# Bank width of ScalarE's softmax reads, and the durations in a list scheduler, in a two-layer attention kernel

## Chip, cores, metric

One core of one Trainium2 chip. The metric is device time in microseconds (us), median of the executions of a kernel. Each ratio compares runs of one job on one chip. One run of the kernel before, of 6325 us (granted clock 1.0), is marked slow and is left out everywhere. PE is the tensor engine, ScalarE is ACT in the profile, VectorE is DVE.

## The reference, cut

```python
def _A_ref(x, wq, wk, wv, wo):             # S=2048, D=512, 32 query heads of 16, one K/V head
    q = split_heads(x @ wq); k = x @ wk; v = x @ wv
    p = softmax(einsum("bhqd,bkd->bhqk", q, k) * 16 ** -0.5)
    return merge(einsum("bhqk,bkd->bhqd", p, v)) @ wo
# _B_ref: linear attention with a feature map phi, 32 heads of 16
x = x + _A_ref(layernorm(x), ...); x = x + _B_ref(layernorm(x), ...)   # this pair twice
```

The two A blocks hold nearly all the work: 2 x 32 x 2048 x 2048 exponentials, which is 4096 score blocks of 128 x 512. The rest (projections, transposes, normalisation, block B) is 222 small jobs per layer that each need a bank, and the kernel slides most of them in between the score blocks.

## The kernel before: the parts that matter

The kernel is built by its own list scheduler. At build time it simulates five engines with a duration for each operation. Whenever an engine is free in that simulation, it takes the ready operation of the best priority. The outcome is a fixed instruction order for each engine, with semaphore waits. That order is fixed in the program: **the durations cost no time, they only shape the order.**

```python
SHARE = True
def tdv(n, c=1.04): return 0.065 + n * c * 1e-3      # VectorE, us for n columns
def tac(n):         return 0.09 + n * 0.833e-3       # ScalarE
```

All matmuls of the profile write to one tensor, `ps_all`, which the kernel allocates in PSUM and divides into eight banks of 512 columns. Banks 0-2 and 3-5 are two "sets" for ScalarE: PE writes a score block into each bank of a set, then one ScalarE exp reads the whole set while PE refills the other. Bank 6 serves both VectorE's score blocks (kind "x") and all small jobs; bank 7 accumulates the output. With `SHARE`, small jobs may also take bank 5, and then the second set is only two banks wide:

```python
# Banks.take(kind), for a small job
elif f[6]: got = 6
elif f[5] and self.share(): got = 5          # share(): SHARE and not ramp and not tail
# Ctl.step(): fill a set
for s in ((0,) if self.ramp else (0, 1)):
    w = 3
    if s == 1 and SHARE and (not banks.free[5] or (not banks.free[6] and self.waiting())):
        w = 2
    ...
# Ctl.fill(): refill by PE, then the exp by ScalarE
o  = add(PE, 0.05 + 0.14 * m, ..., prio=0.0, name="sA")
oe = add(AC, tac(m * 512), lambda e: e.activation(PTA[...], bank(3 * s, m * 512), ACTF.Exp, scale=SCALE), ...)
# Ctl.dstep(): VectorE takes a block farther ahead, if bank 6 is free; if a small job waits, they alternate
if not banks.free[6] or self.dhold(): return False
if self.dlast and self.waiting():     return False
```

So each score block goes to ScalarE (source line L775) or to VectorE (L829 reads bank 6; L846 to L851 make an exp by bit tricks, two blocks at a time), as the simulation decides. Where PE would idle, the scheduler adds filler matmuls (L897).

The softmax here doesn't subtract the row's maximum and nothing guards it: scores larger than these inputs give would overflow.

## Time and profile before

| | before |
|---|---|
| median time | 1849.07 us (3 runs, 1846.9 to 1851.51) |
| busy: PE / ScalarE / VectorE | 95% / 94% / 90% |
| score blocks: ScalarE / VectorE | 3573 / 523 |
| ScalarE exps three / two / one wide | 1039 / 227 / 2 |

Groups by line with shapes kept apart. Columns: count, busy us, mean ns of one as recorded, then the idle time just before them and what ended it.

```profile
L775 ACT ACTIVATE PTA<-ps_all 128x1536 bf16<-128x1536 f32 x1039 | 1437.1, 1478 | 57.6 <-PE ps_all L635 50.7
...
L829 DVE TENSOR_SCALAR xT<-ps_all 128x512 int32<-128x512 f32 x523 | 358.8, 686 | 48.9 <-PE ps_all L635 45.7
...
L775 ACT ACTIVATE PTA<-ps_all 128x1024 bf16<-128x1024 f32 x227 | 235.5, 1038 | 1.7 <-PE ps_all L635 1.4
L897 PE MATMUL ps_all<-maskx,zer 128*128 128x512 bf16 x594 | 205.0, 387 | 0.0
```

The recorded length of an exp (1478 ns on average for three banks) is not what it costs: neighbours overlap. I therefore took, from the trace's records, the time from each exp's start to the next ScalarE instruction's start. At best it is 1330 ns for three banks and 903 ns for two. The means are 1375 and 1171 ns (here and in the tables cut to whole ns). A three-wide exp is usually followed on time (median 1330 ns); one of two banks, on average 268 ns late.

Windows of a burst of small jobs, of a quiet stretch, and of another burst (columns as the first line says):

```profile
core 0: us, PE busy (x) PEld busy (x) DVE busy (x) ACT busy (x) POOL busy (x), PEclk, DMA share, GB/s
450.00:525.00 75.00, 73.54 (x464) 21.64 (x460) 64.74 (x123) 69.38 (x64) 2.60 (x4) 1.00 0.00 1
525.00:650.00 125.00, 119.99 (x709) 31.49 (x709) 118.57 (x200) 120.91 (x92) 0.00 (x0) 1.00 0.00 1
675.00:750.00 75.00, 72.87 (x458) 21.28 (x456) 59.98 (x117) 70.18 (x64) 4.47 (x5) 1.00 0.00 1
```

In the bursts ScalarE is busy 69.4 and 70.2 of 75 us and VectorE only 64.7 and 60.0; in the quiet stretch ScalarE is busy 97% and VectorE 95%. Most two-wide exps lie in bursts. The waits, in us, times and longest, show ScalarE and VectorE each held up by PE's score matmuls:

```profile
engine line waited for: us in total, times, longest us
...
ACT PTA L775 <- PE ps_all L635: 52.1, 127, 1.5
DVE xT L829 <- PE ps_all L635: 45.7, 88, 1.5
```

### The profile page before, as it was taken

The page shows a single profiled execution, that of the slowest core. Times are in us where ns is not written, and L with a number is a line of the kernel's source. Part 1 is how long each engine was busy: PE and PEld are TensorE (multiplying, and loading weights), DVE is VectorE, ACT ScalarE, POOL GpSimd, SP SyncE. Part 2 cuts the span into 40 slices and gives each one's busy share as a digit, 9 for nine tenths or more (in the row PEclk, how much of TensorE's full clock was granted, in tenths as well). Part 3 has the DMA queues.
Part 4 walks back from the last instruction along what each step waited for, and adds up shares of the span by engine and source line. Part 5 has one row for each costly group of instructions (what it writes and reads, how often), then busy time and mean ns, then how long its engine had stood idle before and what let it go on. Part 6 is the DMA issues. An engine that isn't in the chain of part 4 may idle for free.

```text
span 1845.4 us, 26741 instructions
## 1 busy us (share of the span) xinstructions
PE 1754.5 (95%) x11002; PEld 515.1 (28%) x11002; DVE 1658.7 (90%) x2966; ACT 1739.9 (94%) x1529; POOL 34.2 (2%) x46
## 2 busy tenths in 40 slices
PE   7999999999999999999899999999999999999998
PEld 3222222222222222223342222222223222232224
DVE  7999988999889997998689999899997999989985
ACT  7999999999999999999699999999999999999996
POOL 0000000000000000000000000000000000000000
PEclk9999999999999999999999999999999999999999
DMA  3000000000000000000000000000000000000001
GB/s 115 1 1 1 1 1 1 1 1 1 1 1 1 1 1 1 1 1 1 1 1 1 1 1 1 1 1 1 1 1 1 1 1 1 1 1 1 1 1 46
DMA packets 7722, 9.08 MB, mean 5 GB/s; under 512 B 1456, under 2 KB 7088, under 8 KB 7600
## 3 DMA queue, kind: packets, MB, share of 16 engines
q1 hardware_dynamic: 7600, 7.37, 1.2%
q8 instruction: 86, 1.41, 0.3%
q14 instruction: 36, 0.29, 0.1%
HBM read 5.28 MB, written 2.10 MB: 4 GB/s over the span
## 4 chain that ended last, share of the span: by engine, by line
PE 44%; DVE 43%; ACT 11%; issue 1%; POOL 1%; DMA 0%; SPq 0%
PE ps_all L635 17%; PE ps_all L671 13%; ACT PTA L775 10%; DVE xT L829 9%; DVE PTD L851 8%; PE ps_all L496 7%; DVE xs L850 5%; DVE xs L847 5%; DVE xu L846 4%; DVE xu L849 3%; DVE xs L848 2%; PE ps_all L897 2%; PE ps_all L692 1%; DVE Eo L683 1%; DVE stats L461 1%
## 5 line engine op out<-in xcount | busy, mean ns | idle before, releaser
L775 ACT ACTIVATE PTA<-ps_all 128x1536 bf16<-128x1536 f32 (+1 forms) x1268 | 1640.6, 1398 | 59.4 <-PE ps_all L635 52.1
L635 PE MATMUL ps_all<-QT,Kr 64*128 64x512 bf16 x4096 | 835.1, 383 | 42.0 <-DVE xT L829 16.0
L671 PE MATMUL ps_all<-PTA,Vaug 128*32 128x512 bf16 x3573 | 539.3, 389 | 3.4 <-DVE Eo L683 2.8
L829 DVE TENSOR_SCALAR xT<-ps_all 128x512 int32<-128x512 f32 x523 | 358.8, 686 | 48.9 <-PE ps_all L635 45.7
L851 DVE SCALAR_TENSOR_TENSOR PTD<-xT,xs 128x1024 uint16<-128x1024 int32 (+1 forms) x262 | 318.4, 1215 | 1.4
L635 PEld LDWEIGHTS ps_all<-QT,Kr 64*128 64x128 bf16 x4096 | 175.2, 93 | 500.9 <-ACT PTA L775 198.2
L671 PEld LDWEIGHTS ps_all<-PTA,Vaug 128*32 128x32 bf16 x3573 | 129.5, 93 | 463.4 <-issue 451.5
L897 PE MATMUL ps_all<-maskx,zer 128*128 128x512 bf16 x594 | 205.0, 387 | 0.0
L846 DVE TENSOR_SCALAR xu<-xT 128x1024 f16<-128x1024 uint16 (+1 forms) x262 | 180.2, 688 | 3.0
L850 DVE TENSOR_TENSOR xs<-xs,xu 128x1024 f16<-128x1024 f16 (+1 forms) x262 | 179.0, 684 | 3.0
L847 DVE TENSOR_TENSOR xs<-xu 128x1024 f16<-128x1024 f16 (+1 forms) x262 | 178.7, 682 | 2.0
L671 PE MATMUL ps_all<-PTD,Vaug 128*32 128x512 bf16 x523 | 144.3, 385 | 16.4 <-DVE Eo L683 12.9
L848 DVE TENSOR_SCALAR xs<-xs 128x1024 f16<-128x1024 f16 (+1 forms) x262 | 109.6, 418 | 2.1
L849 DVE TENSOR_SCALAR xu<-xu 128x1024 f16<-128x1024 f16 (+1 forms) x262 | 109.5, 418 | 0.0
L897 PEld LDWEIGHTS ps_all<-maskx,zer 128*128 128x128 bf16 x594 | 48.7, 96 | 105.0 <-issue 98.3
L496 PE MATMUL ps_all<-wqkv_sb,xnT 128*128 128x512 bf16 x256 | 70.9, 383 | 3.3 <-DVE xnT L485 1.1
L469 POOL TENSOR_TENSOR rstd<-veps,mhalf 128x1 f32<-128x1 f32 x30 | 30.7, 1025 | 1731.1 <-DVE veps L467 1723.3
L940 DVE TENSOR_SCALAR e_buf<-e_buf 128x512 f32<-128x512 f32 x64 | 26.9, 422 | 32.8 <-ACT e_buf L939 32.5
L671 PEld LDWEIGHTS ps_all<-PTD,Vaug 128*32 128x32 bf16 x523 | 32.3, 94 | 65.3 <-DVE Eo L683 27.7
L692 PE MATMUL ps_all<-identf,Eo 128*128 128x128 f32 x256 | 42.0, 287 | 5.6 <-DVE Eo L683 4.0
L939 ACT ACTIVATE e_buf<-ps_all 128x512 f32<-128x512 f32 x64 | 39.0, 610 | 8.3 <-PE ps_all L496 6.1
L461 DVE BATCH_NORM_STATS2 stats<-x_sb 128x6 f32<-128x512 bf16 x64 | 43.2, 683 | 3.3 <-DMA x_sb<-in_A_x_dram 2.6
(87 smaller groups left out, 841.6 us busy)
## 6 DMA issues: line engine op xcount, KB each, us to landing
out_dram<-x_sb SPq DMA_DIRECT2D x16, 128.0 KB, 1.7
x_sb<-in_A_x_dram SPq DMA_DIRECT2D x3, 512.0 KB, 6.7
wqkv_sb<-in_B_wqkv_dram SPq DMA_DIRECT2D x1, 1536.0 KB, 11.6
x_sb<-in_A_x_dram SPq DMA_DIRECT2D x2, 256.0 KB, 3.1
wq_sb<-in_A_wq_dram SPq DMA_DIRECT2D x1, 512.0 KB, 4.6
wo_sb<-in_A_wo_dram SPq DMA_DIRECT2D x1, 512.0 KB, 8.5
wo_sb<-in_B_wo_dram SPq DMA_DIRECT2D x1, 512.0 KB, 10.9
wk_sb<-in_A_wk_dram SPq DMA_DIRECT2D x1, 16.0 KB, 2.6
```

The lines of the kernel that those rows point to most:

```text
L496: i = e.matmul(bank(h.idx, n), lhsT=l, rhs=r, start=(c + k == 0), stop=(c + k == len(mms) - 1))
L635: x = e.matmul(bank(b0 + k), lhsT=Kr[r, m, kt * P:(kt + 1) * P], rhs=QT[r, self.units[u][0] % 2, gs, q0:q0 + n], start=True, stop=True)
L671: return e.matmul(ps[32 * c:32 * c + 32, 7 * 512:8 * 512], lhsT=Vaug[:, kt, :], rhs=src, start=opened[0], stop=opened[1], skip_group_check ...
L775: oe = add(AC, tac(m * 512), lambda e: e.activation(PTA[:, hp.idx, 0:m * 512], bank(3 * s, m * 512), ACTF.Exp, scale=SCALE), deps=[o] + pr ...
L829: o = add(DV, tdv(512), lambda e: e.tensor_scalar(out=xT[:, hx.idx, i * 512:(i + 1) * 512], in0=bank(6), scalar1=SCALE * LOG2E * 65536.0, ...
L846: o = add(DV, tdv(w, 0.52), lambda e: e.tensor_scalar(out=u_, in0=lo, scalar1=1.0 / 65536, scalar2=-0.5, op0=ALU.mult, op1=ALU.add), deps= ...
L847: o1 = add(DV, tdv(w, 0.52), lambda e: e.tensor_tensor(out=s_, in0=u_, in1=u_, op=ALU.mult), deps=[o] + c["prev"], name="xsq", **kw)
L848: o2 = add(DV, tdv(w, 0.26), lambda e: e.tensor_scalar(out=s_, in0=s_, scalar1=XK, scalar2=-XW, op0=ALU.mult, op1=ALU.add), deps=[o1], nam ...
L849: o3 = add(DV, tdv(w, 0.26), lambda e: e.tensor_scalar(out=u_, in0=u_, scalar1=1.0, scalar2=XL, op0=ALU.mult, op1=ALU.add), deps=[o1], nam ...
L850: o4 = add(DV, tdv(w, 0.52), lambda e: e.tensor_tensor(out=s_, in0=s_, in1=u_, op=ALU.mult), deps=[o2, o3], name="xc", **kw)
L851: o5 = add(DV, tdv(w), lambda e: e.scalar_tensor_tensor(out=PTD[:, hp.idx, 0:w].bitcast(U16), in0=xT[:, k, 0:w], scalar=2.0 ** -9, in1=s_, ...
L897: o = add(PE, 0.03 + FILLN * 0.41e-3, lambda e: e.matmul(bank(7, FILLN), lhsT=zer[:], rhs=maskx[:].bitcast(BF16)[:, 0:FILLN], start=not ow ...
```

## The change

Its intent: ScalarE always reads three banks (bank 5 is no longer lent), and the scheduler's durations are set to what the chip shows. `tac` is the duration of an exp and of ScalarE's few small operations. The core of the diff:

```diff
-    SHARE = True
+    SHARE = False
-        return 0.065 + n * c * 1e-3          # tdv, VectorE
+        return 0.068 + n * c * 1e-3
-        return 0.09 + n * 0.833e-3           # tac, ScalarE
+        return 0.0525 + n * 0.8325e-3
 # and seven lines with single durations, cut: bn_aggr 0.18 -> 0.09; veps 0.14 -> 0.062; transposed copies 0.4 -> 0.333 (twice);
 # K evacuation +0.06 (VectorE) and +0.1 (ScalarE); reciprocal 0.246 -> 0.168; zb 0.13 -> 0.195
```

More of the change, by code (lines that the diff above doesn't have):

```diff
@@ L461, in layer_norm @@
         add(DV, tdv(512), lambda e: e.bn_stats(stats[:, t, 0:6], x_sb[:, t, :]), reads=[("x", t)], writes=[("st", t)], prio=prio, name="bn")
-        add(DV, 0.18, lambda e: e.bn_aggr(mv[:, t, :], stats[:, t, 0:6]), reads=[("st", t)], writes=[("mv", t)], prio=prio - 0.01)
+        add(DV, 0.09, lambda e: e.bn_aggr(mv[:, t, :], stats[:, t, 0:6]), reads=[("st", t)], writes=[("mv", t)], prio=prio - 0.01)
         if ctl.ramp or ctl.tail:
@@ L466, in layer_norm @@
         else:
-            add(DV, 0.14, lambda e: e.tensor_scalar(out=veps[:, t:t + 1], in0=mv[:, t, 1:2], scalar1=1e-5, scalar2=None, op0=ALU.add),
+            add(DV, 0.062, lambda e: e.tensor_scalar(out=veps[:, t:t + 1], in0=mv[:, t, 1:2], scalar1=1e-5, scalar2=None, op0=ALU.add),
                 reads=[("mv", t)], writes=[("ve", t)], prio=prio - 0.02)
@@ L485, in cp @@
             return f(xnT[:, :, t * P:(t + 1) * P], bank_bf(hb.idx))
-        o2 = add((DV, AC), {DV: 0.4, AC: tac(512)}, cp, deps=[o], uses=[hb], rel=[hb] + ([win] if win else []), writes=[("xnT", t)], prio=prio - 0.04, name="xnT", cb=cb)
+        o2 = add((DV, AC), {DV: 0.333, AC: tac(512)}, cp, deps=[o], uses=[hb], rel=[hb] + ([win] if win else []), writes=[("xnT", t)], prio=prio - 0.04, name="xnT", cb=cb)
     def proj(h, mms, n, reads, prio, chunk=2, name="proj"):
@@ L513, in k_proj @@
                 ops = {}
-            ops[m] = add((DV, AC), {DV: tdv(b - a), AC: tac(b - a)}, ev, deps=[o] + ([ops[m - 1]] if m else []), uses=[h], rel=[h] if m == NM - 1 else [],
+            ops[m] = add((DV, AC), {DV: 0.06 + tdv(b - a), AC: 0.1 + tac(b - a)}, ev, deps=[o] + ([ops[m - 1]] if m else []), uses=[h], rel=[h] if m == NM - 1 else [],
                          reads=["mpar"], writes=[("K", m, t) for t in range(t0, t0 + n)], prio=prio - 0.05, name="kev")
@@ L694, in norm @@
             o = add(PE, 1.0, tr, reads=["identf"], deps=[oe], acq=[ht, hos] if par == 0 else [ht], uses=[he], rel=[he], prio=1.2, name="trA")
-            o = add(DV, 0.246, lambda e: e.reciprocal(rden[:, hr.idx, :].unsqueeze(2), bank(ht.idx).rearrange("p (a c) -> p a c", c=32)[:, :, DH:DH + 1]),
+            o = add(DV, 0.168, lambda e: e.reciprocal(rden[:, hr.idx, :].unsqueeze(2), bank(ht.idx).rearrange("p (a c) -> p a c", c=32)[:, :, DH:DH + 1]),
                     deps=[o], acq=[hr], uses=[ht], prio=0.0, name="recA")
@@ L921, in cp @@
             return fn(OT[:, :, g, :] if fine else OT[:, g, :, :], bank_bf(h.idx))
-        o2 = add((DV, AC), {DV: 0.4, AC: tac(512)}, cp, deps=[o], uses=[h], rel=[h], writes=keys, prio=pr, name="otc")
+        o2 = add((DV, AC), {DV: 0.333, AC: tac(512)}, cp, deps=[o], uses=[h], rel=[h], writes=keys, prio=pr, name="otc")
         if fine:
@@ L1021, in kv_block @@
                 for g in (2 * hh, 2 * hh + 1):
-                    add(DV, tdv(P, 0.52), lambda e, g=g: e.tensor_scalar(out=zb[:, g, :], in0=maskx[:, 0:P], scalar1=zf[:, g:g + 1], scalar2=None, op0=ALU.mult),
+                    add(DV, 0.195, lambda e, g=g: e.tensor_scalar(out=zb[:, g, :], in0=maskx[:, 0:P], scalar1=zf[:, g:g + 1], scalar2=None, op0=ALU.mult),
                         reads=[("zf", hh), "mask"], writes=[("zb", g)], prio=0.75, name="zb")
```

## The prediction

> **What bounds the kernel now.** Every softmax score block (128x512; 4096 of them) is exponentiated either by ScalarE (L775) or by VectorE (six ops and an L829 read). The groups by form show 1039 ScalarE exps three banks wide, 227 two wide, 2 one wide (3573 blocks) and 523 blocks on VectorE. The page shows ScalarE busy 94%, VectorE 90%, PE 95%, but 594 of PE's matmuls (205 us busy) are filler, so PE has room except in bursts. The kernel is a shared ScalarE/VectorE throughput problem: in quiet stretches (e.g. 525 to 650 us) ScalarE is 97% and VectorE 95% busy and about 2.56 blocks finish per us; in bursts of projection/epilogue work (450 to 525, 675 to 750 us, and their like in layer 2) only about 2.1 per us, with VectorE 80 to 86% busy. Most two-wide exps lie in those bursts.
>
> **Costs.** In the trace, back-to-back exps start 1330 ns apart when three wide, 903 ns when two wide. That is 51 ns + 0.833 ns per column[...]. So the fixed cost alone is little: 443 against 452 ns per block, 4 us in all. But starts after a two-wide exp really follow by 1171 ns on average (1375 for three wide): 0.9 us is too short for PE to refill the other set. Effective cost per block: 585 against 458 ns. The 454 blocks of two-wide exps take 266 us of ScalarE; three wide they would take 208. Gain 58 us of ScalarE time.
>
> **What it costs.** Bank 5 no longer serves projections, transposes and epilogues; all that work shares bank 6 with VectorE's score blocks. Mapping instructions to the kernel's banks, in layer 1's stream (50 to 850 us) bank 6 is held 555 us (351 by 248 VectorE blocks of 1.4 us, 204 by other work), bank 5 by other work 204 us. Unchanged, the sum would fill 95% of bank 6 before hand-offs. Holds should shrink with one job in flight, but in bursts VectorE gets one block per job, so bursts stretch, and VectorE gives up an estimated 15 to 60 of its 490 streaming blocks; ScalarE takes each at 458 ns. With 40 lost: 3613 blocks, 1204 exps at about 1365 ns = 1644 us against 1698 now: 54 us saved. PE refills more evenly, fillers rise.
>
> **Durations.** They change no instruction's cost, only order and split. The old model held an exp 38 ns too long (1.370 against 1.330), so the plan made ScalarE wait slightly and gave VectorE too much; I credit a few us, within the 1365.
>
> **On the critical path.** Nearly all of it: ScalarE time per block sets the pace. I take off about 15 us for backlog at layer ends (850 to 930 us and after 1775 us, where few blocks flow), and imperfect refills. Net 38 us.
>
> **Predicted: 1811 us, range 1783 to 1843. Faster by over 2%: 0.50; within 2%: 0.46; slower: 0.04.**
>
> **What would show it.** Two-wide exps: 227 to nearly 0 (ramp and end only); three-wide about 1200; VectorE blocks 460 to 510; mean start-to-start of three-wide exps 1355 to 1375 ns; VectorE idle up (waits of L829 for PE, 46 us, rise); bursts longer but ScalarE above 96% busy in them; ramp, layer change (about 850 to 940 us) and last 70 us unchanged within 10 us.
>
> **What would make it wrong.** VectorE starves far more (under 420 blocks), cancelling the gain; a QT projection delayed past its deadline stalls the score stream; the exps' waits come from PE's order, not from width, so three-wide exps in bursts also start late (over 1400 ns); or, better than expected, the right durations remove the exps' lateness and lift VectorE too (below 1783 us).

1644 us of exps against 1698 make 54 saved, less about 15 for layer ends and refills, so net 38 off 1849, or 1811 us. The 51 ns itself is what the trace leaves: 1330 ns less 0.833 x 1536.

## More of the kernel before

From the profile's page of the kernel before: the span, the busy times, and the engines' shares in the chain of work that ended last.

```profile
span 1845.4 us, 26741 instructions
...
PE 1754.5 (95%) x11002; PEld 515.1 (28%) x11002; DVE 1658.7 (90%) x2966; ACT 1739.9 (94%) x1529; POOL 34.2 (2%) x46
...
PE 44%; DVE 43%; ACT 11%; issue 1%; POOL 1%; DMA 0%; SPq 0%
```

A piece of ScalarE's timeline inside a burst, merged, with the idle time ahead in brackets:

```profile
start us, us, engine line op out<-in xcount [idle before <-releaser]
482.15 2.37 ACT L775 ACTIVATE PTA<-ps_all 128x1536 bf16<-128x1536 f32 x2 [0.26 <-PE ps_all L635]
485.26 3.93 ACT L775 ACTIVATE PTA<-ps_all 128x1536 bf16<-128x1536 f32 x3 [0.75 <-PE ps_all L635]
489.09 0.59 ACT L939 ACTIVATE e_buf<-ps_all 128x512 f32<-128x512 f32 x1
489.57 3.29 ACT L775 ACTIVATE PTA<-ps_all 128x1024 bf16<-128x1024 f32 x3
```

A merged line names only the shape of its first instruction; the records show that widths alternate in all these lines. There are two gaps of 0.26 and 0.75 us in 4 us, each after a two-wide exp and each ended by PE's score matmuls: that is what lateness looks like.

The experiments took four jobs on four chips, in which the median of the kernel before was 1848.3 to 1850.2 us, so a difference between kernels of different jobs is good to about 2 us.

## The result

| | before | changed |
|---|---|---|
| median time | 1849.94 us (4 runs) | 1804.30 us (4 runs, 1800.92 to 1805.22) |
| ratio, 95% interval | | 0.9752, 0.9733 to 0.977 |
| busy: PE / ScalarE / VectorE | 95 / 94 / 90% | 95 / 97 / 85% |
| score blocks: ScalarE / VectorE | 3573 / 523 | 3632 / 464 |
| three-wide exps, mean start to start | 1039, 1375 ns | 1208, 1365 ns |
| two-wide exps, mean start to start | 227, 1171 ns | 4, 1698 ns |

A ratio is the mean time of one kernel's runs over that of the other's in the same rounds, so it is not quite the ratio of the medians.

The profile after; first the page's lines.

```profile
span 1803.5 us, 26242 instructions
...
PE 1715.0 (95%) x10931; PEld 502.9 (28%) x10931; DVE 1541.4 (85%) x2728; ACT 1743.8 (97%) x1472; POOL 35.1 (2%) x46
...
ACT 49%; PE 31%; DVE 18%; issue 1%; POOL 1%; DMA 0%; SPq 0%
```

The chain has turned: ScalarE held 11% of it before and 49% now. Groups by form:

```profile
L775 ACT ACTIVATE PTA<-ps_all 128x1536 bf16<-128x1536 f32 x1208 | 1648.5, 1529 | 15.8 <-PE ps_all L635 13.6
...
L829 DVE TENSOR_SCALAR xT<-ps_all 128x512 int32<-128x512 f32 x464 | 318.3, 686 | 106.3 <-PE ps_all L635 105.1
...
L897 PE MATMUL ps_all<-maskx,zer 128*128 128x512 bf16 x523 | 170.3, 386 | 0.0
```

The two-wide group is all but gone. ScalarE's idle time before its three-wide exps fell from 57.6 to 15.8 us; VectorE's before its reads of bank 6 rose from 48.9 to 106.3 us. Windows of similar stretches (the columns are those shown above):

```profile
450.00:525.00 75.00, 71.60 (x439) 19.20 (x437) 63.23 (x115) 74.24 (x58) 4.14 (x4) 1.00 0.00 1
525.00:575.00 50.00, 48.34 (x318) 14.11 (x316) 38.30 (x67) 49.91 (x41) 0.00 (x0) 1.00 0.00 1
575.00:650.00 75.00, 72.09 (x441) 19.05 (x439) 70.22 (x117) 74.39 (x56) 0.00 (x0) 1.00 0.00 1
675.00:750.00 75.00, 72.46 (x468) 20.74 (x465) 62.78 (x110) 74.46 (x59) 1.54 (x2) 1.00 0.00 1
```

ScalarE is now busy over 74 of 75 us inside what used to be bursts, and the small jobs are spread: VectorE is also short of work from 525 to 575 us, which was quiet before. Waits and a piece of ScalarE's timeline:

```profile
DVE xT L829 <- PE ps_all L635: 105.1, 163, 1.7
...
ACT PTA L775 <- PE ps_all L635: 13.6, 38, 1.5
```

```profile
481.72 1.45 ACT L775 ACTIVATE PTA<-ps_all 128x1536 bf16<-128x1536 f32 x1
483.06 0.59 ACT L939 ACTIVATE e_buf<-ps_all 128x512 f32<-128x512 f32 x1
483.54 5.49 ACT L775 ACTIVATE PTA<-ps_all 128x1536 bf16<-128x1536 f32 x4
489.35 10.90 ACT L775 ACTIVATE PTA<-ps_all 128x1536 bf16<-128x1536 f32 x8 [0.32 <-PE ps_all L635]
```

Fourteen ScalarE instructions in a row, with one gap of 0.32 us.

Where did the 42 us of the two profiled spans go? Summing start-to-start times over all exps gives ScalarE's time for exps with the waits behind them: 1697.9 us before, 1656.4 after, a difference of 41.5. So it is there. This sum is the yardstick of the experiments.

### The profile page after: what moved, and what is told of

Same layout as the page of the kernel before. It is cut to its first block, busy times and chain, and to the rows that moved or that the text cites. A ratio compares the mean times of both kernels' runs of the same rounds, so it can differ in the third digit from the quotient of the medians.

```text
span 1803.5 us, 26242 instructions
## 1 busy us (share of the span) xinstructions
PE 1715.0 (95%) x10931; PEld 502.9 (28%) x10931; DVE 1541.4 (85%) x2728; ACT 1743.8 (97%) x1472; POOL 35.1 (2%) x46
## 4 chain that ended last, share of the span: by engine, by line
ACT 49%; PE 31%; DVE 18%; issue 1%; POOL 1%; DMA 0%; SPq 0%
ACT PTA L775 47%; PE ps_all L635 13%; PE ps_all L671 8%; PE ps_all L496 5%; DVE xT L829 3%; DVE PTD L851 3%; PE ps_all L897 2%; DVE xu L846 2%; DVE xs L847 1%; DVE xs L850 1%; DVE stats L461 1%; ACT e_buf L939 1%; PE ps_all L1060 1%; DVE xu L849 1%; DVE Eo L683 1%; DVE xs L848 1%
## 5 line engine op out<-in xcount | busy, mean ns | idle before, releaser
L775 ACT ACTIVATE PTA<-ps_all 128x1536 bf16<-128x1536 f32 (+1 forms) x1212 | 1652.4, 1528 | 15.8 <-PE ps_all L635 13.6
L829 DVE TENSOR_SCALAR xT<-ps_all 128x512 int32<-128x512 f32 x464 | 318.3, 686 | 106.3 <-PE ps_all L635 105.1
L851 DVE SCALAR_TENSOR_TENSOR PTD<-xT,xs 128x1024 uint16<-128x1024 int32 x232 | 282.3, 1217 | 2.3
L897 PE MATMUL ps_all<-maskx,zer 128*128 128x512 bf16 x523 | 170.3, 386 | 0.0
L846 DVE TENSOR_SCALAR xu<-xT 128x1024 f16<-128x1024 uint16 x232 | 159.8, 689 | 4.4
L847 DVE TENSOR_TENSOR xs<-xu 128x1024 f16<-128x1024 f16 x232 | 158.8, 685 | 3.8
L850 DVE TENSOR_TENSOR xs<-xs,xu 128x1024 f16<-128x1024 f16 x232 | 158.7, 684 | 3.1
L671 PE MATMUL ps_all<-PTD,Vaug 128*32 128x512 bf16 x464 | 120.9, 387 | 9.0 <-DVE Eo L683 5.7
L848 DVE TENSOR_SCALAR xs<-xs 128x1024 f16<-128x1024 f16 x232 | 96.8, 417 | 2.6
L849 DVE TENSOR_SCALAR xu<-xu 128x1024 f16<-128x1024 f16 x232 | 96.9, 418 | 0.0
L683 DVE COPY Eo<-ps_all 128x512 f32<-128x512 f32 x62 | 42.5, 685 | 2.9 <-PE ps_all L671 1.6
```

The source lines that it names most:

```text
L671: return e.matmul(ps[32 * c:32 * c + 32, 7 * 512:8 * 512], lhsT=Vaug[:, kt, :], rhs=src, start=opened[0], stop=opened[1], skip_group_check ...
L775: oe = add(AC, tac(m * 512), lambda e: e.activation(PTA[:, hp.idx, 0:m * 512], bank(3 * s, m * 512), ACTF.Exp, scale=SCALE), deps=[o] + pr ...
L829: o = add(DV, tdv(512), lambda e: e.tensor_scalar(out=xT[:, hx.idx, i * 512:(i + 1) * 512], in0=bank(6), scalar1=SCALE * LOG2E * 65536.0, ...
L846: o = add(DV, tdv(w, 0.52), lambda e: e.tensor_scalar(out=u_, in0=lo, scalar1=1.0 / 65536, scalar2=-0.5, op0=ALU.mult, op1=ALU.add), deps= ...
L847: o1 = add(DV, tdv(w, 0.52), lambda e: e.tensor_tensor(out=s_, in0=u_, in1=u_, op=ALU.mult), deps=[o] + c["prev"], name="xsq", **kw)
L848: o2 = add(DV, tdv(w, 0.26), lambda e: e.tensor_scalar(out=s_, in0=s_, scalar1=XK, scalar2=-XW, op0=ALU.mult, op1=ALU.add), deps=[o1], nam ...
```

## The experiments

Theory W, that of the prediction: the gain comes from width. Theory D, the rival: it comes from the durations; the old plan held an exp for 1.370 us where the chip starts the next one after 1.330, so all orders were made for a ScalarE that is too slow.

| kernel | median us | ratio to before | three-wide | two-wide | VectorE blocks | exp sum, us | ScalarE's share of the chain |
|---|---|---|---|---|---|---|---|
| before | 1849.9 | 1 | 1039 x 1375 ns | 227 x 1171 ns | 523 | 1697.9 | 11% |
| flag only | 1817.5 | 0.9823 | 1206 x 1381 | 2 | 472 | 1671.4 | 19% |
| all durations only | 1829.8 | 0.9892 | 1044 x 1359 | 225 x 1145 | 514 | 1677.3 | 36% |
| ScalarE's duration only | 1821.8 | 0.985 | 1038 x 1356 | 232 x 1131 | 516 | 1673.6 | 33% |
| flag + ScalarE's duration | 1799.8 | 0.9731 | 1212 x 1361 | 2 | 456 | 1652.3 | 61% |
| changed | 1804.3 | 0.9752 | 1208 x 1365 | 4 | 464 | 1656.4 | 49% |
| flag, exp 37.5 ns too short | 1799.0 | 0.9728 | 1214 x 1351 | 4 | 445 | 1646.2 | 84% |
| flag, exp 75 ns too long | 1855.2 | 1.003 | 1201 x 1417 | 3 | 485 | 1708.6 | 7% |
| changed, set two always 2 wide | 1880.0 | 1.0168 | 731 x 1344 | 714 x 1043 | 474 | 1729.7 | 30% |
| the same, bank 5 lent | 1857.8 | 1.0044 | 718 x 1345 | 703 x 1054 | 536 | 1707.5 | 25% |

Against before, each kernel's profiled span moved by what its exp sum moved, within 3.6 us (examples: flag only -28.9 and -26.5; set two always 2 wide +32.3 and +31.8). All results were correct. The share of the chain does not rank the kernels: the one of 1880 us has 30%, the one of 1817.5 us 19%.

The scheduler's own end times are worth a look (found by running the scheduler in each kernel's source, without the chip): 1816.5 us before, 1815.6 with the flag alone, 1776.6 with the flag and ScalarE's duration, 1734.0 with the exp too short, 1858.1 with it too long. The simulation sees almost nothing of the 32 us that the flag gave on the chip, and for the too short exp it promises another 43 us, which the chip did not give.

### share_only: the flag alone

```diff
-    SHARE = True
+    SHARE = False
```

> Only the flag: every ScalarE exp takes three banks, all durations of the scheduler as before. Theory W (width: two-wide exps were too short for PE to refill, 585 against 458 ns per block) expects most of the gain here: 1803 to 1820 us, about 1200 three-wide exps, 470 VectorE blocks. Theory D (durations: the plan held an exp 38 ns too long, so every engine followed a plan that was too slow) expects 1838 to 1850 us, with three-wide exps starting late on average (mean start-to-start over 1385 ns).

Measured 1817.46 us, ratio 0.9823 (0.981 to 0.9836): inside W's range, and the larger part of the gain. But three-wide starts followed after 1381 ns: D's mark (over 1385) was just missed, yet that is later than before (1375), while the prediction had counted on 1365. The page's span and chain:

```profile
span 1816.5 us, 26252 instructions
...
DVE 40%; PE 38%; ACT 19%; issue 2%; POOL 0%; DMA 0%; SPq 0%
```

With two-wide exps gone, ScalarE still did not pace the kernel: VectorE and PE held 78% of the chain.

### dur_only and tac_only: durations, flag as before

`dur_only` takes all durations of the diff. `tac_only` takes one line:

```diff
-        return 0.09 + n * 0.833e-3
+        return 0.0525 + n * 0.8325e-3
```

> Only the durations, the flag as before (bank 5 still lent to other work, some 225 two-wide exps). W expects 1835 to 1848 us, with a two-wide exp still followed only after about 1150 ns. D expects 1803 to 1815 us, with start-to-start after a two-wide exp nearer 1000 ns.

> Only ScalarE's duration (51 ns + 0.8325 ns per column in place of 90 + 0.833), nothing else. W expects 1838 to 1849 us. D expects the same as with all durations within 5 us, since the exps are the only long ScalarE work: 1803 to 1818 us.

Measured 1829.75 us (0.9892) and 1821.76 us (0.985). Both theories missed: the times are 5 and 16 us below W's ranges and 15 and 4 us above D's. ScalarE's duration alone did better than all durations, by 8 us, where D had wanted both within 5. Two-wide exps stayed slow, at 1145 and 1131 ns, as W had it; three-wide ones came 16 and 19 ns sooner than before (1359 and 1356). So the effects are two, they are of similar size, and they overlap: flag 32 us and duration 28 us alone, 50 together; on top of the duration, the flag gave 22.

### share_tac: the flag and ScalarE's duration

> The flag and ScalarE's duration, the small VectorE durations (bn_aggr, reciprocal, transposed copies, K evacuation) as before. Both theories expect the changed kernel's time within 6 us (1798 to 1810 us): the small durations sum to about 64 x (0.09 + 0.078) + 96 x 0.067 = 17 us of VectorE plan time, and VectorE is not what sets the pace.

The edit is the two diffs above together. Measured 1799.84 us (0.9731), as expected, and it is a little faster than the changed kernel. Its page:

```profile
span 1798.1 us, 26055 instructions
...
ACT 61%; PE 25%; DVE 13%; issue 1%; DMA 0%; SPq 0%
```

ScalarE holds 61% of the chain. After the flag, one duration took another 17.6 us with not one instruction made cheaper.

### exp_short and exp_long: how a wrong duration acts

On the base of `share_tac`:

```diff
-        return 0.0525 + n * 0.8325e-3
+        return 0.015 + n * 0.8325e-3     # exp_short
+        return 0.1275 + n * 0.8325e-3    # exp_long
```

> The flag, and ScalarE's durations in the plan another 37.5 ns too short (15 ns fixed in place of 52.5, which is what the chip shows). If the gain from the duration is that the plan agrees with the chip (theory T), this is no better or worse: 1798 to 1815 us, and VectorE's chain gets late instead. If it is only that PE refills the sets earlier in its order (theory P), the wait from an exp's recorded end to the refill falls below 223 ns, three-wide starts follow after less than 1361 ns, and the time falls to 1785 to 1796 us.

> The flag, with ScalarE's plan duration 75 ns longer than the chip's (127.5 ns fixed in place of 52.5; the kernel before had 90, which gave 1817.5 us, and 52.5 gave 1799.8). If too long an exp in the plan is what makes PE refill late (theory P), the refill wait rises beyond 368 ns, three-wide starts follow after 1395 to 1420 ns, VectorE takes about 485 blocks, and the time is 1830 to 1850 us. If the step from 1817 to 1800 was luck of the order, it stays within 1800 to 1825 us.

Measured 1798.99 us (0.9728) and 1855.22 us (1.003). Four kernels now differ in this one number (to within 0.8 ns at 1536 columns). "Refill wait" is the median time from an exp's recorded end to the first weight load of the score matmuls that refill its set, from the trace's records:

| fixed term in the plan | 127.5 ns | 90 | 52.5 | 15 |
|---|---|---|---|---|
| refill wait | 488 ns | 368 | 223 | 98 |
| three-wide start to start | 1417 ns | 1381 | 1361 | 1351 |
| VectorE blocks | 485 | 472 | 456 | 445 |
| time | 1855.2 us | 1817.5 | 1799.8 | 1799.0 |

The pages of the two extremes, too long first:

```profile
span 1853.6 us, 26454 instructions
...
DVE 52%; PE 38%; ACT 7%; issue 2%; DMA 0%; POOL 0%; SPq 0%; another core or an unknown queue 0%
```

```profile
span 1797.3 us, 25990 instructions
...
ACT 84%; PE 11%; DVE 4%; issue 0%; DMA 0%; SPq 0%; ACTq 0%
```

The traces agree with the mechanism of P: the longer an exp is in the plan, the later stands its refill in PE's order, behind work that waits for VectorE (52% of the chain in the slow kernel, 4% in the fast one). It can be seen in who waits for whom. First the slow kernel, then the fast one:

```profile
PEld ps_all L635 <- ACT PTA L775: 109.3, 314, 1.1
...
PEld ps_all L635 <- DVE xT L829: 62.2, 125, 1.4
ACT PTA L775 <- PE ps_all L635: 46.5, 138, 0.8
```

```profile
PEld ps_all L635 <- ACT PTA L775: 340.8, 845, 1.2
DVE xT L829 <- PE ps_all L635: 112.8, 183, 1.4
...
ACT PTA L775 <- PE ps_all L635: 3.8, 14, 0.3
```

In the fast kernel PE comes to the score matmuls early and its weight loads (PEld) wait for ScalarE to finish, 341 us in all; in the slow one only 109 us, and VectorE holds them up for longer (62 us, against 21 in the fast one). There ScalarE is done early and waits for PE, 46.5 us against 3.8.

But P's times were wrong at both ends. Too long cost more than expected (1855 against 1830 to 1850). Too short gained nothing (1799 against 1785 to 1796), as T had it: exps came 10 ns sooner, but VectorE, starved by the same order (its wait for PE was 112.8 us, against 95.6 in `share_tac`), did 11 blocks fewer, which ScalarE had to do.

### w32_noshare and w32_bank5: width and bank, one at a time

On the base of the changed kernel:

```diff
-                w = 3
+                w = 2 if s == 1 and not self.ramp else 3             # both kernels
-    banks.share = lambda: SHARE and not ctl.ramp and not ctl.tail
+    banks.share = lambda: True and not ctl.ramp and not ctl.tail     # w32_bank5 only
```

> The changed kernel, but the second bank set is always read two wide once the ramp is over, and bank 5 stays unused: width alone, with nothing gained from the bank. In the kernel before, a three-wide set is refilled in at least 51 + 640 ns after the earlier exp's recorded end, which is 148 ns after its slot ends: 839 ns in all, against 1330 ns under a three-wide exp and 903 ns under a two-wide one. Theory W expects start-to-start after a two-wide exp of 1050 to 1200 ns, not 903, so 2.4 us or more per five blocks, and 1840 to 1880 us in all. If width costs only its fixed 51 ns (rival), the loss is about 700 x 30 ns, i.e. 1815 to 1830 us.

> The second set always two wide, as in the last width run (1880 us), but now bank 5 is lent to projections, transposes and epilogues at all times: what a second bank for other work is worth alone. If bank 6 holds VectorE back in bursts (theory B), VectorE blocks rise from 474 to 510 or more and the time falls by 15 to 35 us, to 1845 to 1865 us. If VectorE's blocks are limited elsewhere, 1872 to 1885 us.

Measured 1880.03 us (1.0168), at the very top of W's range, and 1857.82 us (1.0044). Width alone costs 76 us against the changed kernel; the rival's 1815 to 1830 is out. The groups of the first:

```profile
L775 ACT ACTIVATE PTA<-ps_all 128x1536 bf16<-128x1536 f32 x731 | 1073.7, 1469 | 60.7 <-PE ps_all L635 54.0
...
L775 ACT ACTIVATE PTA<-ps_all 128x1024 bf16<-128x1024 f32 x714 | 747.0, 1046 | 0.3
```

ScalarE idles 60.7 us here, nearly all of it before three-wide exps. That is the sign of the theory: a refill takes at least 839 ns (148 + 51 + 640, as expected above), 491 ns less than a three-wide exp lasts and only 64 ns less than a two-wide one. So 0.9 us is not too short for every refill, but it has hardly any slack: of the two-wide exps 40% were followed more than 50 ns late, of the three-wide ones 4% (the median two-wide one was followed on time, after 904 ns). The lateness after two-wide exps adds up to 100 us, after three-wide ones to 10; the 234 exps more, at 51 ns, are only 12 us. Start to start after a two-wide exp was 1043 ns, just under the expected range. Per block that is 521 ns against 448. It is better than the 1171 of the kernel before. A second small job in flight is not the reason by itself, for the next run has one and shows 1054; the kernel before had its two-wide exps in bursts only, and a plan with too long exps, and I did not separate these. With bank 5 put back into the set, which is all that the changed kernel has more, the idle time falls from 60.7 to 15.8 us.

Lending bank 5 gave back 22 us and 62 VectorE blocks (474 to 536). Waits without and with the bank:

```profile
DVE xT L829 <- PE ps_all L635: 106.7, 164, 1.4
...
ACT PTA L775 <- PE ps_all L635: 54.0, 145, 1.1
```

```profile
ACT PTA L775 <- PE ps_all L635: 59.5, 144, 1.1
DVE xT L829 <- PE ps_all L635: 50.0, 98, 1.8
```

VectorE's wait for its score blocks halves. So bank 6 does hold VectorE back, and the flag's price is real: it is smaller than the gain from width.

### nudge_up, nudge_down, hold_both: noise of the plan, and a try at better

On the base of `share_tac`: VectorE's fixed 65 ns as 66 and as 64, which should mean nothing; and a change of priorities.

```diff
-        return 0.065 + n * c * 1e-3
+        return 0.066 + n * c * 1e-3      # nudge_up; 0.064 in nudge_down
```

```diff
 # hold_both: later matmuls of a projection, and the feature map's two VectorE ops
-            o = add(PE, ..., f, reads=reads, prio=prio, ...)
+            o = add(PE, ..., f, reads=reads, prio=prio if c == 0 else min(prio, 1.4), ...)
-  ... prio=prio, name="phm")   /   prio=prio - 0.1, name="phf")
+  ... prio=0.6, name="phm")    /   prio=0.5, name="phf")
```

> The kernel with the flag and ScalarE's duration, and every VectorE duration 1 ns longer in the plan, which is nothing in itself. If the order that the scheduler finds reacts to nothings (theory J), the time moves by several us, as much as the 4.5 us that the small durations cost on top: 1796 to 1808 us, away from 1799.8. If the order is stable (theory S), 1799.8 within 1.5 us, and the small durations really cost 4.5 us.

> As the last, with every VectorE duration 1 ns shorter. J: again several us away from 1799.8, in either direction; S: within 1.5 us of it.

> The flag and ScalarE's duration (1799.8 us), with the later matmuls of a projection and VectorE's two feature-map ops put ahead of other work in the plan's priorities, so that a projection lets go of bank 6 sooner. If bank 6 limits VectorE in bursts (theory B), the mean hold of the pk and pq projections falls from about 4.4 to 3.5 us, VectorE takes 465 or more blocks and the time is 1788 to 1797 us. If holds do not matter, or PE's order suffers, 1798 to 1806 us.

The nudges took 1800.26 and 1797.49 us (0.9735, 0.9722). Neither theory is clean: one lies within S's 1.5 us, one just outside, and neither is several us away as J said. About 2 us is what the order moves by itself, and part of that goes with the granted clock (0.998 in most runs of `nudge_up`, 1.0 in most of `nudge_down`; at 0.999 one run of each took 1799.1 and 1799.4), so `share_tac`, the nudges and `exp_short` are the same to me.

`hold_both` took 1802.28 us (0.9743), no better. Its means failed: from the records, the pk projection held bank 6 in layer 1's stream for about 4.1 us, as in `share_tac` (4.0), and pq for 4.2 against 3.8; only the output projection and block B's v projection let go sooner (1.9 us each, against 2.2 and 2.3). Some matmul records are missing in both traces (the page of `share_tac` has 10780 matmuls and 10936 weight loads), so these are good to about 0.2 us. (The 4.4 us expected as the start is the hold in the changed kernel.) VectorE took 458 blocks, not 465. So this run says nothing on whether shorter holds would help; it only shows that these priorities do not shorten them.

### changed_again: where 4.5 us went

> The changed kernel again, unaltered. Its four first runs had mean granted clocks of 0.996 to 0.999, and the one at 0.999 took 1800.9 us against 1803.7 to 1805.2 of the others; the profiled one lost 10 us to half clock in one burst. If the 4.5 us by which it trails the kernel without the small VectorE durations (1799.8 us, clock 0.999 to 1.000) are that clock (theory C), runs at 0.999 or 1.000 take 1798 to 1802 us and runs at 0.996 to 0.997 take 1803 to 1806. If they are the small durations (theory V), runs at 0.999 or 1.000 still take 1803 us or more.

Measured 1801.65 us (0.9747). Five runs: 1801.03 and 1800.92 at a mean granted clock of 0.999, 1801.65 at 0.998, 1802.71 at 0.997 (0.3 us under C's range for it), 1805.84 at 0.996. Taken with the first job's runs, the three at 0.999 took 1800.9 to 1801.0, where `share_tac` at 0.999 took 1799.8 to 1801.3. Theory V is out: without lending bank 5, the small durations cost nothing that can be seen. Windows of the changed kernel in the first profile, where the clock fell (columns as in the windows above):

```profile
255.00:258.40 3.40, 3.40 (x21) 0.94 (x20) 2.51 (x5) 3.40 (x4) 0.00 (x0) 1.00 0.00 0
258.40:261.80 3.40, 2.05 (x17) 0.49 (x16) 3.37 (x6) 3.40 (x5) 0.00 (x0) 1.00 0.00 0
261.80:272.00 10.20, 10.20 (x40) 2.18 (x37) 4.53 (x9) 7.01 (x5) 0.00 (x0) 0.50 0.01 2
272.00:278.00 6.00, 6.00 (x45) 1.71 (x42) 3.11 (x4) 5.46 (x5) 0.00 (x0) 1.00 0.00 0
```

PE was busy for 2.05 of 3.40 us, then the granted clock was 0.50 for 10.2 us, although the profile has PE busy all through, and ScalarE was busy for only 7.01 of those. From 1159.5 to 1162.9 us of the same trace it was 0.50 too, with ScalarE busy for 2.97 of 3.40 us. Half of these 13.6 us is 6.8 of 1803.5, which is the mean of 0.996. What made the clock fall is not shown.

What stays open: with the flag as before, all durations were 8 us slower than ScalarE's alone (1829.8 against 1821.8, all at clock 1.000). That is more than the nudges moved anything; I did not find which duration does it.

## Why the prediction was right, and where it was not

The time, 1804.3 us, lies in the range, and the predicted gain of 38 us was 46 in the medians. Point by point:

- **Width is a large part: right, but it is not nearly all.** The flag alone gave 32 us, and forcing two-wide exps cost 76; on top of ScalarE's duration the flag gave 22. The mechanism given (0.9 us is too short for a refill) held in a weaker form: 0.9 us leaves a refill 64 ns of slack.
- **VectorE gives up 15 to 60 blocks: right.** It gave up 59, its wait for PE went from 46 to 105 us, and lending a bank without any change of width gave 62 back.
- **Counts and paces of the changed kernel: right.** 1208 three-wide exps, 464 VectorE blocks, 1365 ns.
- **"I credit a few us, within the 1365" for the durations: wrong, by far the largest miss.** The step to 1365 ns was ascribed to PE refilling more evenly once all sets are three wide. The flag alone made three-wide exps later (1381). It was ScalarE's duration that brought 1361. That duration was worth 17.6 us after the flag and 28 alone; all durations of the change together were worth 13 (16 by `changed_again`) and 20. The prediction had the right direction ("the plan made ScalarE wait slightly") and the wrong size for it.
- **"ScalarE time per block sets the pace": not so before.** The chain of waits of the kernel before gave ScalarE 11%, PE 44% and VectorE 43%. I did not use that view. It said that ScalarE was following PE's order; only with the right duration or a shorter one, and the flag, does ScalarE hold the largest part of the chain (49 to 84%).
- **Saved ScalarE time 54 us, less 15 for backlog at layer ends: both too large.** Exps took 1656 us, not 1644, for VectorE gave up 59 blocks and not 40 (19 x 0.455 = 9 us), and four two-wide exps took 1.7 us each. From the records, the pause between the layers' exps grew from 35.7 to 40.0 us and the end after the last exp from 40.6 to 42.4: 6 us and not 15. ScalarE's other instructions between the exps took 6 us less, so outside the exp sum the span did not change at all (147.5 us before, 147.1 after).
- **The nearness of 1811 to 1804 is in part luck.** The exp term was 12.5 us too large and the allowance 15 us, and the two cancel. The flag alone ended at 1817.5 us, in the range too, but only 1.8% faster; that the kernel came out over 2% faster, to which the prediction gave 0.50, it owes to the durations that were credited with a few us.
- **Fillers would rise: wrong.** They fell from 594 to 523. That is not the flag: the scheduler adds 591 with the flag alone (counted by running it) and 528 with ScalarE's duration too.

The fixed cost of 51 ns agrees with the trace: 1330 and 903 ns less 0.833 ns x 1536 and x 1024 leave 51 and 50. The 0.833 stood in the kernel's own `tac`; in the trace 512 columns more take 427 ns, 0.834 each.

## What to carry to other kernels

When an instruction order is made from modelled durations, take them from start-to-start times in the trace: an exp planned 38 ns too long, of 1330, cost 18 to 28 us in 1850, by putting other engines' instructions in the wrong order; planned 75 ns too long it cost 55 us (1855.2 against 1799.8), and 37.5 ns too short, nothing. When two buffers alternate, compare the refill's latency with the time of the *shorter* occupant (here 839 with 903 ns); a smaller tile that costs nearly the same per element (452 against 443 ns per block) can still stall its neighbour. And before calling an engine the bottleneck because it is 94% busy, read its share of the chain that ended last: not as a measure of speed, but to see whose order it follows.
